# Turning four row sums by transposing transfers instead of TensorE

## Chip, core and metric

The kernel runs on one core of a Trainium2 chip. The metric is the device time of one execution in microseconds; the number before is the median of three runs. Engines: PE (TensorE), DVE (VectorE), ACT (ScalarE), POOL (GpSimd) and SP (SyncE), which here only issues transfers. PEld is TensorE's weight load.

## What is computed

```python
x  = A_q                                   # 1 x 2048 x 1024, float32
xn = layernorm(x)                          # over the 1024 columns
conv = long causal convolution of (short causal convolution of k) * v, per channel, plus a skip term
ffn  = silu(xn @ w1) @ w2                  # w1 1024 x 3584, w2 3584 x 1024
out  = x + xn * conv + ffn
```

The feed-forward part is nearly all of TensorE's work. The convolution is done by Fourier transforms (small matmuls on TensorE, butterflies on DVE).

## The kernel before, in words

Float32 products are made of three float16 products: each operand is split into a high half (ACT writes it) and a low rest (DVE writes it); this pair of instructions is the helper `split`. Lines L359 (ACT) and L351 (DVE) are helper lines through which all of these run.

The first matmul takes x in two row halves of 1024 rows. For most columns of w1 it uses a recursive scheme with seven products instead of eight (`PRODUCTS`). Its left operands are quarters of the normalised x, turned so that columns lie on partitions (`A11`, `A12`, `A21`, `A22`), and four sums of them, `S1` to `S4`. Each lies in one place `x0` to `x7` in SBUF as four row parts of 128 x 512: `S3` in x7, `S2` in x6, `S1` in x0, `S4` in x1, `A11` in x2, `A12` in x3, `A21` in x4, `A22` in x5.

For the first row half, `x_rows` adds the sums in place on DVE: row tiles xt4 to xt7 become `S3` and `S1`, then xt0 to xt3 become `S2` and `S4`. `transposes` turns each 128 x 512 part by four TensorE transposes into a PSUM tile `ft` (three of them in a ring), from which `split` writes high and low halves into the place. For the second half, `more_sums` splits the rows as they lie into a buffer `s`, `spill` stores them in DRAM (`xsp...`), and `load_x` reads them back much later by a transposing transfer (`X`, L341).

The order of all instructions is made when the program is built, by a list scheduler (`Order`). Generators yield operations with an estimated length; at each step the one with the earliest start minus its stream's bias is emitted. Each engine, and SP's queue, then runs its own list in order. `feed_forward` is one generator, so TensorE's matmuls of that part have a fixed sequence: two "plain" column blocks on the first half (48 matmuls of 256 columns with four row parts each, then 48 of 512), the same two blocks on the lower quarters (96 matmuls of 512 columns), then units of seven products of 12 matmuls. The products of the first unit go in the order P1 (`A11`), P7 (`S3`), P6 (`S2`), P2 (`A12`), P5 (`S1`), P1 of the next unit, P3 (`S4`), P4 (`A22`).

```python
PRODUCTS = {"P1": ("A11", "B11"), "P7": ("S3", "T3"), "P6": ("S2", "T2"), "P2": ("A12", "B21"),
            "P5": ("S1", "T1"), "P3": ("S4", "B22"), "P4": ("A22", "T4")}
XPLACE = dict(A11=2, A12=3, A22=5, S1=0, S2=6, S3=7, S4=1)
```

The right operands come from w1: `raw` tiles are loaded, their squares summed on ACT, factors formed on DVE and split into the ring `wo`.

Of the kernel before, what the change touches and what calls it, by code (L numbers as in the profile page):

```python
# [13 lines left out]
F16 = mybir.dt.float16  # L14
# [6 lines left out]
P = 128  # L21
# [6 lines left out]
KH = KD // 2  # L28
# [7 lines left out]
XS = 512.0  # L36
# [21 lines left out]
NC = len(PLAIN) // 4  # L58
W2PLACE = [(2, 6, 4, 0, 3), (1, 5, 7, 2, 6)]
FPLACE = (4, 0, 3, 1, 5, 7, 2, 6)  # L60

FACTORS = (("B11",), ("T2", "T3"), ("B21", "B22"), ("T4", "T1"))

# [53 lines left out]
class Order:  # L117
# [27 lines left out]
    def add(self, gen, bias, floor=0.0):  # L145
        s = Stream(gen, bias, floor)
        self.streams.append(s)
        self.advance(s)
# [151 lines left out]
def h3_ffn_kernel(ctx, tc, x, kp, vs, fs, shift, dskip, w1, w2, cfwd, cinv, out):  # L300
# [3 lines left out]
    add = order.add  # L304
    flag = defaultdict(Token)
# [12 lines left out]
    def size(a):  # L318
        n = 1
        for s in a.shape[1:]:  # L320
            n *= s
        return n
# [7 lines left out]
    def T(f, o, ins, us, m=0.1):  # L330
        return Op("PE", us, 0.3, f, ins, [o], m)
# [2 lines left out]
        n = size(o) * o.shape[0] * mybir.dt.size(o.dtype)  # L334
        return Op("SP", 0.4, 0.1, lambda: nc.sync.dma_start(o, i), [i], [o], m, n)

    def X(o, i, m=0.3):

        n = size(o) * o.shape[0] * mybir.dt.size(o.dtype)
        k = 1.2 if i.space == bass.MemoryType.DRAM else 3.0  # L340
        return Op("SP", 0.65 + n / 240e3, 0.1, lambda: nc.sync.dma_start(o, i, transpose=True), [i], [o], m, k * n)  # L341

    def G(o, i, m=0.3):
# [3 lines left out]
    def v_tt(o, a, b, op, **k):  # L347
        return V(lambda: nc.vector.tensor_tensor(o, a, b, op=op), o, [a, b], **k)  # L348

    def v_stt(o, a, s, b, op0, op1, **k):  # L350
        return V(lambda: nc.vector.scalar_tensor_tensor(o, a, s, b, op0=op0, op1=op1), o,  # L351
                 [a, b] + ([] if isinstance(s, float) else [s]), **k)

    def a_act(o, i, func, scale=1.0, bias=None, total=None):
        def f():
            kw = {} if bias is None else {"bias": bias}
            if total is not None:
                kw["accum_out"] = total
            nc.scalar.activation(o, i, func, scale=scale, **kw)  # L359
        ins = [i] + [s for s in (scale, bias) if s is not None and not isinstance(s, float)]  # L360
        p = A(f, o, ins)
        p.table = func if func in (AF.Silu, AF.Sqrt) else None
        p.busy += 0.07 * (len(ins) - 1) - 0.06 * (i.space == bass.MemoryType.PSUM)
        if total is not None:
            p.busy += 0.19
            p.writes.append(total)
        return p

    def split(hi, lo, src, scale, after=()):

        yield a_act(hi, src, AF.Copy, scale)
        yield v_stt(lo, src, scale, hi, MUL, SUB)
        for t in after:
            t.set()
# [56 lines left out]
    xst_r = Halves(order, lnp, "s", 6)  # L431
# [79 lines left out]
    xts, xns, xo = {}, {}, [{}, {}]  # L511
# [71 lines left out]
    def factor(name):  # L583

        if name == "A21":
            return second["A21"]
        return xo[0][name]

    def turned(src, tok, name, i, bias):

        yield ft.ready
        pt, ptok = ft.tile([P, KH, P])

        def mm():
            for c in range(KH):
                nc.tensor.transpose(pt[:, c, :], src[:, c * P:(c + 1) * P], ident)  # L596
        yield T(mm, pt, [src], 0.44, m=0.3)
        flag["turned", name, i].set()
        if tok is not None:
            tok.set()  # L600
        o = factor(name)[:, i]
        after = (ptok, flag["x", 0, name]) + ((flag["rows", i],) if name in ("A11", "A12") else ())
        add(split(o[:, :, 0], o[:, :, 1], pt, XS, after), bias)

    def transposes():
        for n, name in enumerate(("A11", "A12")):
            xo[0][name], xtok[0][name] = places[XPLACE[name]].tile([P, 4, KH, 2, P], F16)
        for i in range(4):
            yield flag["xn", i]
            x, _ = xns[i]  # L610
            yield from turned(x[:, 0:W], None, "A11", i, 0.2)
            yield from turned(x[:, W:], None, "A12", i, 0.2)
        second["A21"], second["tok"] = places[4].tile([P, 4, KH, 2, P], F16)
        for name in ("A22", "S2", "S3", "S1", "S4"):
            r = places[XPLACE[name]]
            yield r.ready
            xo[0][name], xtok[0][name] = r.tile([P, 4, KH, 2, P], F16)
        for i in range(4):
            yield flag["xn", 4 + i]
            z, _ = xns[4 + i]  # L620
            yield from turned(z[:, 0:W], None, "A21", i, 0.14)
            yield from turned(z[:, W:], None, "A22", i, 0.14)
        for name, low, q in (("S3", 4, 0), ("S2", 0, 0), ("S1", 4, 1), ("S4", 0, 1)):
            for i in range(4):
                yield flag["summed", name, i]
                x, tok = xns[low + i]
                yield from turned(x[:, q * W:(q + 1) * W], tok, name, i, 0.11)

    def x_rows():
        for i in range(4):  # L630
            for name in ("A21", "A22"):
                yield flag["turned", name, i]
            x, z = xns[i][0], xns[4 + i][0]
            yield v_tt(z[:, W:], z[:, 0:W], z[:, W:], ADD)
            flag["summed", "S1", i].set()
            yield v_tt(z[:, 0:W], x[:, 0:W], z[:, 0:W], SUB)
            flag["summed", "S3", i].set()
        for i in range(4):
            x, z = xns[i][0], xns[4 + i][0]
            yield v_tt(x[:, 0:W], z[:, W:], x[:, 0:W], SUB)  # L640
            flag["summed", "S2", i].set()
            yield v_tt(x[:, W:], x[:, W:], x[:, 0:W], SUB)
            flag["summed", "S4", i].set()
        yield 0.02
        for i in range(4):
            yield from more_sums(i)
        flag["x done"].set()
# [303 lines left out]
    def steps(o, w, xf, first, last, more=False):  # L951

        for k in range(KH):
            def mm(k=k):
                kw = dict(skip_group_check=more)
                nc.tensor.matmul(o, w[:, 0, k], xf[:, :, k, 0], start=first and k == 0, stop=False, **kw)  # L956
                nc.tensor.matmul(o, w[:, 0, k], xf[:, :, k, 1], start=False, stop=False, **kw)  # L957
                nc.tensor.matmul(o, w[:, 1, k], xf[:, :, k, 0], start=False, stop=last and k == KH - 1, **kw)  # L958
            yield T(mm, o, [w[:, :, k], xf[:, :, k]], 3 * (size(o) / 2400 + 0.003))
# [343 lines left out]
    def norms_w2():  # L1303
# [18 lines left out]
        for h in range(2):  # L1322
            for c in range(NC):
# [6 lines left out]
                for a in (0, 2):  # L1330
                    i = PLAIN[4 * c + a] // 2
                    raw, tok = yield from next_w2()
                    add(split(wc[:, a:a + 2, 0, :], wc[:, a:a + 2, 1, :], raw, tau[:, i:i + 1], (tok, flag["w2", h, c])), 0.05)
        yield places[FPLACE[0]].ready
        hold, ktok = places[FPLACE[0]].tile([P, NQ, W], F32)
        at = iter(FPLACE[1:])

# [602 lines left out]
```

## Time and profile before

| | |
|---|---|
| median of 3 runs | 1242.98 us (1242.75 to 1246.18) |
| profiled execution | 1248.08 us, span 1246.2 us |
| PE busy | 1233.9 us (99%) |
| DVE busy | 1108.8 us (89%) |
| ACT busy | 777.4 us (62%) |
| mean granted TensorE clock | 0.998 |
| moved by DMA | 275.62 MB, mean 221 GB/s |

The profile is of a single execution. Rows of a timeline give start, length, engine, line, operation and tiles; brackets hold the idle time just before an instruction and what ended it. Ends of matmuls are modelled: back to back, matmuls of 512 columns start every 0.216 us though each is listed with 0.38 us. Rows by stretch give, for each engine, busy time and the number of instructions, then the granted clock, the share of the DMA engines' time and GB/s.

### The profile page before, as it was taken

To read this page: it belongs to the slowest core of one execution; us is meant where nothing else is said; L and a number is where in the kernel's file an instruction comes from. 1 tells how busy PE (TensorE), PEld (TensorE's weight loads), DVE (VectorE), ACT (ScalarE), POOL (GpSimd) and SP (SyncE) were. 2 spreads that over 40 slices of the span, in tenths; PEclk is the share of its full clock that TensorE was granted. 3 is DMA by queue.
4 is the path that set the end of the run, shared out by engine and by line. 5 is a ranking of instruction groups with operands and counts; after the bars stand their busy time and mean duration, and the time that the engine had idled before them with its cause. 6 is when DMAs were issued, how large, how long until landed. Compare 5 with 4: busy or idle time off the path is not lost.

```text
span 1246.2 us, 16970 instructions
## 1 busy us (share of the span) xinstructions
PE 1233.9 (99%) x6092; PEld 602.5 (48%) x6092; DVE 1108.8 (89%) x1252; ACT 777.4 (62%) x1361; POOL 83.3 (7%) x93
## 2 busy tenths in 40 slices
PE   9999999999999999999999999999999999999998
PEld 8544444444444544445444544544454454445444
DVE  7999987997999769998899799889979979997992
ACT  7768987886687977559743732654273374545233
POOL 0000000000000000000000000000030130113114
PEclk9999999999999999999999999999999999999999
DMA  9368889789999888869986466389576766787777
GB/s 366 102 229 275 310 306 333 234 256 222 258 337 290 254 284 286 240 188 298 299 280 176 121 224 178 110 261 308 131 140 193 177 126 185 184 167 115 167 137 102
DMA packets 265028, 275.62 MB, mean 221 GB/s; under 512 B 72944, under 2 KB 191984, under 8 KB 263664
## 3 DMA queue, kind: packets, MB, share of 16 engines
q1 hardware_dynamic: 249216, 258.02, 67.2%
q0 software_dynamic: 15728, 16.52, 10.3%
q8 instruction: 47, 0.77, 0.3%
q14 instruction: 37, 0.30, 0.1%
HBM read 171.46 MB, written 88.34 MB: 208 GB/s over the span
## 4 chain that ended last, share of the span: by engine, by line
PE 87%; DVE 7%; DMA 3%; ACT 2%; issue 1%; SPq 0%; DVEq 0%; ACTq 0%
PE ff L956 13%; PE ff L957 13%; PE ff L958 13%; PE ff L1099 13%; PE ff L1101 13%; PE ff L1100 13%; DVE spec L348 2%; PE ps L1601 2%; DMA wraw<-in_w 2%; PE ps L1603 2%; PE ps L1602 2%; DVE tmp L348 1%; DVE x L351 1%; PE ft L596 1%; PE py L1790 1%
## 5 line engine op out<-in xcount | busy, mean ns | idle before, releaser
L1099 PE MATMUL ff<-x,wo 128*128 128x512 f16 x868 | 328.1, 378 | 1.5 <-ACT hf L359 0.7
L1101 PE MATMUL ff<-x,wo 128*128 128x512 f16 x868 | 328.1, 378 | 0.0
L1100 PE MATMUL ff<-x,wo 128*128 128x512 f16 x868 | 328.1, 378 | 0.0
L956 PE MATMUL ff<-x,wo 128*128 128x512 f16 (+1 forms) x808 | 303.3, 375 | 0.0
L957 PE MATMUL ff<-x,wo 128*128 128x512 f16 (+1 forms) x808 | 303.1, 375 | 0.0
L958 PE MATMUL ff<-x,wo 128*128 128x512 f16 (+1 forms) x808 | 303.1, 375 | 0.0
L348 DVE TENSOR_TENSOR spec<-spec 128x1024 f32<-128x1024 f32 (+2 forms) x232 | 259.4, 1145 | 2.1
L1101 PEld LDWEIGHTS <-wo 128*128 128x128 f16 x868 | 84.9, 98 | 101.6
L1099 PEld LDWEIGHTS <-wo 128*128 128x128 f16 x868 | 85.8, 99 | 99.2
L1100 PEld LDWEIGHTS <-wo 128*128 128x128 f16 x868 | 84.9, 98 | 101.1 <-issue 2.2
L958 PEld LDWEIGHTS <-wo 128*128 128x128 f16 x808 | 79.1, 98 | 92.4 <-issue 0.6
L956 PEld LDWEIGHTS <-wo 128*128 128x128 f16 x808 | 80.6, 100 | 88.2 <-issue 0.7
L957 PEld LDWEIGHTS <-wo 128*128 128x128 f16 x808 | 79.1, 98 | 88.3 <-issue 0.7
L348 DVE TENSOR_TENSOR tmp<-spec 128x2048 f32<-128x2048 f32 (+1 forms) x48 | 92.4, 1932 | 0.9
L359 ACT ACTIVATE spec<-spec 128x1024 bf16<-128x1024 f32 x32 | 33.7, 1054 | 68.5 <-DVE spec L348 68.5
L351 DVE SCALAR_TENSOR_TENSOR ht<-hf,wsc,ht 128x1024 f16<-128x1024 f32 (+1 forms) x56 | 67.4, 1203 | 10.0 <-ACT ht L359 9.7
L351 DVE SCALAR_TENSOR_TENSOR sig<-kin,taps,sig 128x1024 f32<-128x1024 f32 x48 | 61.4, 1280 | 12.0 <-ACT sig L359 12.0
L351 DVE SCALAR_TENSOR_TENSOR wo<-raw,wsc,wo 128x1024 f16<-128x1024 f32 (+1 forms) x56 | 64.0, 1146 | 8.7 <-ACT wo L359 8.6
L359 ACT ACTIVATE wo<-raw,wsc 128x1024 f16<-128x1024 f32 (+1 forms) x56 | 57.9, 1034 | 13.5 <-DVE raw L348 8.2
L345 POOL DMA_DIRECT2D out<-hf x44 | 39.5, 903 | 344.8 <-ACT hf L359 201.1
L359 ACT ACTIVATE ht<-hf,wsc 128x1024 f16<-128x1024 f32 (+1 forms) x56 | 60.8, 1086 | 2.0 <-DMA hsfA<-ht 0.3
L348 DVE TENSOR_TENSOR spec<-tmp 128x512 f32<-128x512 f32 (+1 forms) x80 | 60.7, 793 | 1.0
(187 smaller groups left out, 1707.3 us busy)
## 6 DMA issues: line engine op xcount, KB each, us to landing
wo<-hs SPq DMA_DIRECT2D x160, 256.0 KB, 3.5
hs<-ht SPq DMA_DIRECT2D x80, 256.0 KB, 4.5
raw<-in_w SPq DMA_DIRECT2D x28, 512.0 KB, 5.5
wraw<-in_w SPq DMA_DIRECT2D x24, 512.0 KB, 5.8
w2n<-in_w SPq DMA_DIRECT2D x24, 512.0 KB, 6.6
ws_T<-wo SPq DMA_DIRECT2D x22, 512.0 KB, 5.4
kin<-in_kp SPq DMA_DIRECT2D x16, 704.0 KB, 6.2
wo<-ws_T SPq DMA_DIRECT2D x22, 512.0 KB, 4.6
```

Source lines behind the costliest of these rows:

```text
L345: return Op("POOL", 1.1, 3.0, lambda: nc.gpsimd.dma_start(o, i, accum_op=ADD), [i], [o], m, 2.3 * n)
L348: return V(lambda: nc.vector.tensor_tensor(o, a, b, op=op), o, [a, b], **k)
L351: return V(lambda: nc.vector.scalar_tensor_tensor(o, a, s, b, op0=op0, op1=op1), o, [a, b] + ([] if isinstance(s, float) else [s]), **k)
L359: nc.scalar.activation(o, i, func, scale=scale, **kw)
L956: nc.tensor.matmul(o, w[:, 0, k], xf[:, :, k, 0], start=first and k == 0, stop=False, **kw)
L957: nc.tensor.matmul(o, w[:, 0, k], xf[:, :, k, 1], start=False, stop=False, **kw)
L958: nc.tensor.matmul(o, w[:, 1, k], xf[:, :, k, 0], start=False, stop=last and k == KH - 1, **kw)
L1099: nc.tensor.matmul(po, hx[:, n, 0, :], wc[:, n, 0, :], start=first and n == 0, stop=False, **kw)
L1100: nc.tensor.matmul(po, hx[:, n, 0, :], wc[:, n, 1, :], start=False, stop=False, **kw)
L1101: nc.tensor.matmul(po, hx[:, n, 1, :], wc[:, n, 0, :], start=False, stop=last and n == 3, **kw)
L1601: nc.tensor.matmul(o, cf[:, 0], h, start=i == 0, stop=False, **kw)
L1602: nc.tensor.matmul(o, cf[:, 0], l, start=False, stop=False, **kw)
```

## The change

`transposes` skips all four sums. `x_rows` instead adds a stream `shipped` for each row tile after its sums: it splits the whole row of two sums (128 x 1024) into a buffer `s` with rows on partitions, and `across` then turns each sum's part by one transposing transfer from SBUF to its place in SBUF. The streams have biases of 0.2 (`S3`), 0.15 (`S2`) and 0.1. The estimate of such a transfer's length can now be given by the caller.

```diff
+SHIPPED = ('S3', 'S1', 'S2', 'S4')
+URGENT = dict(S3=0.2, S2=0.15)
...
-    def X(o, i, m=0.3):
+    def X(o, i, m=0.3, k=None):
...
-        k = 1.2 if i.space == bass.MemoryType.DRAM else 3.0
+        k = k or (1.2 if i.space == bass.MemoryType.DRAM else 3.0)
...
         for name, low, q in (("S3", 4, 0), ("S2", 0, 0), ("S1", 4, 1), ("S4", 0, 1)):
+            if name in SHIPPED:
+                continue
             for i in range(4):
...
+    def shipped(names, i, src, toks):
+
+        def steps():
+            yield xst_r.ready if len(names) == 1 else xst_r.pairs
+            rows, rtok = (xst_r.tile if len(names) == 1 else xst_r.pair)([P, len(names) * KH, 2, P], F16, len(names))
+            yield from split(rows[:, :, 0], rows[:, :, 1], src.rearrange("p (k w) -> p k w", w=P), XS, toks)
+            for n, name in enumerate(names):
+                add(across(name, i, rows[:, n * KH:(n + 1) * KH], rtok), URGENT.get(name, 0.1))
+        add(steps(), URGENT.get(names[0], 0.1))
+
+    def across(name, i, rows, tok):
+
+        yield lambda: name in xo[0]
+        yield X(xo[0][name][:, i].rearrange("p k h w -> p (k h) w"), rows.rearrange("p k h w -> p (k h w)"), k=1.5)
+        tok.set()
+        flag["x", 0, name].set()
...
             flag["summed", "S3", i].set()
+            shipped(('S3', 'S1'), i, z, (xns[4 + i][1],) * 2)
...
             flag["summed", "S4", i].set()
+            shipped(('S2', 'S4'), i, x, (xns[i][1],) * 2)
```

Because the scheduler lays everything out anew, the order moves on every engine. Three places matter below.

TensorE, from the norm of a w1 tile (nm) to the first plain block on the lower quarters (ff1 from x4). Before:

```order
L489 MATMUL nm_656<-ss0_442,one_155 128x2
L596 MATMUL ft0_678<-ident_157,xt7_251 128x128 x4
L596 MATMUL ft1_686<-ident_157,xt7_251 128x128 x4
L596 MATMUL ft2_693<-ident_157,xt4_240 128x128 x4
L596 MATMUL ft0_705<-ident_157,xt5_244 128x128 x4
L956 LDWEIGHTS wo0_172
L956 MATMUL ff1_708<-x4_471,wo0_172 128x512
```

The same place now:

```order
L492 MATMUL nm_659<-ss0_442,one_155 128x2
L599 MATMUL ft0_684<-ident_157,xt7_251 128x128 x4
L599 MATMUL ft1_693<-ident_157,xt7_251 128x128 x4
L980 LDWEIGHTS wo0_172
L980 MATMUL ff1_707<-x4_471,wo0_172 128x512
```

Two transpose groups of `S3` (rows xt4 and xt5) stood ahead of the block; the other fourteen stood between its matmuls and those of the three blocks after it. All sixteen are gone.

DVE, at the same time: evacuations of `ft` to x4 and x5, the row additions, and now the split of a whole row into s1. Before:

```order
L348 TENSOR_TENSOR xt6_248<-xt2_225,xt6_248 128x512
L348 TENSOR_TENSOR xt7_251<-xt7_251 128x512
L351 SCALAR_TENSOR_TENSOR x4_471<-ft0_678,x4_471 128x4x128
L351 SCALAR_TENSOR_TENSOR x5_472<-ft1_686,x5_472 128x4x128
L348 TENSOR_TENSOR xt7_251<-xt3_228,xt7_251 128x512
L348 TENSOR_TENSOR xt0_201<-xt4_240,xt0_201 128x512
```

Now:

```order
L351 TENSOR_TENSOR xt6_248<-xt6_248 128x512
L354 SCALAR_TENSOR_TENSOR x4_471<-ft0_684,x4_471 128x4x128
L354 SCALAR_TENSOR_TENSOR x5_472<-ft1_693,x5_472 128x4x128
L354 SCALAR_TENSOR_TENSOR s1_193<-xt5_244,s1_193 128x8x128
L351 TENSOR_TENSOR xt6_248<-xt2_225,xt6_248 128x512
L351 TENSOR_TENSOR xt7_251<-xt7_251 128x512
```

The last evacuation to x4 comes after fewer additions, but the split into s0 (not in this piece) has moved ahead of the evacuations before it, and more splits stand between the additions.

SP's queue, between the first store of finished blocks (hs0) and the second pair of w1 loads (raw0). Before, with the stores of w1 factors (ws2) between:

```order
L335 DMA hs0_73<-ht1_182 128x4x256 x2
L335 DMA xt4_820<-in_x 128x1024
L335 DMA ws2_B11_77<-wo1_173 128x1024
L335 DMA xt5_852<-in_x 128x1024
L335 DMA xt6_861<-in_x 128x1024
L335 DMA xt7_869<-in_x 128x1024
L335 DMA ws2_T2_78<-wo4_176 128x2048
L335 DMA ws2_B21_79<-wo5_177 128x2048
L335 DMA hs1_74<-ht0_181 128x4x256 x2
L335 DMA raw0_942<-in_w1 128x4x256
```

Now (the last seven of the sixteen transposing transfers, and what is behind them):

```order
L344 DMA_TRANSPOSE x6_473<-s5_197 128x8x128
L344 DMA_TRANSPOSE x1_581<-s4_196 128x8x128
L344 DMA_TRANSPOSE x6_473<-s0_192 128x8x128
L344 DMA_TRANSPOSE x1_581<-s5_197 128x8x128
L344 DMA_TRANSPOSE x6_473<-s1_193 128x8x128
L344 DMA_TRANSPOSE x1_581<-s0_192 128x8x128
L344 DMA_TRANSPOSE x1_581<-s1_193 128x8x128
L338 DMA hs0_73<-ht1_182 128x4x256 x2
L338 DMA hs1_74<-ht0_181 128x4x256 x2
L338 DMA xt7_764<-in_x 128x1024
L338 DMA raw0_869<-in_w1 128x4x256
```

The transfer that completes `S2` (x6 from s1) is the fourteenth of the sixteen; two stores, a row load and the w1 loads stand behind the last.

## The prediction

> **What bounds the kernel now.** I read the page first, then the busy time by stretch.
>
> ```profile
> span 1246.2 us, 16970 instructions
> PE 1233.9 (99%) x6092; PEld 602.5 (48%) x6092; DVE 1108.8 (89%) x1252; ACT 777.4 (62%) x1361; POOL 83.3 (7%) x93
> ```
>
> ```profile
> core 0: us, PE busy (x) PEld busy (x) DVE busy (x) ACT busy (x) POOL busy (x), PEclk, DMA share, GB/s
> 20.00:40.00 20.00, 20.00 (x147) 14.70 (x145) 18.15 (x46) 19.81 (x33) 0.00 (x0) 1.00 0.86 311
> 40.00:60.00 20.00, 18.48 (x108) 11.04 (x106) 19.79 (x33) 13.79 (x27) 0.00 (x0) 1.00 0.16 36
> 60.00:80.00 20.00, 20.00 (x110) 10.96 (x108) 19.30 (x32) 15.11 (x27) 0.00 (x0) 1.00 0.90 293
> ...
> 400.00:500.00 100.00, 97.89 (x474) 46.55 (x472) 80.90 (x91) 80.79 (x147) 0.00 (x0) 0.98 0.85 276
> 1200.00:1246.00 46.00, 41.39 (x227) 21.97 (x225) 20.98 (x26) 17.64 (x34) 16.72 (x17) 0.98 0.71 107
> ```
>
> TensorE (PE) sets the time: it is idle for only 1246.2 - 1233.9 = 12.3 us, of which 4.6 lie at the very end. Work taken from it is time won, unless it waits instead. The work removed lies in 40 to 70 us, where DVE is nearly full too (19.8 and 19.3 of 20) and DMA almost empty at first (0.16). So whether DVE and the transfers deliver the sums in time decides.
>
> **The change, part by part.** The groups of instructions of the first 260 us, shapes apart, give the prices (xcount, busy us, mean ns, idle before):
>
> ```profile
> L351 DVE SCALAR_TENSOR_TENSOR x<-ft,x 128x512 f16<-128x512 f32 x32 | 20.3, 681 | 0.5 <-ACT x L359 0.5
> L359 ACT ACTIVATE x<-ft 128x512 f16<-128x512 f32 x32 | 17.4, 592 | 3.1 <-PE ft L596 2.8
> L351 DVE SCALAR_TENSOR_TENSOR s<-xt,s 128x1024 f16<-128x1024 f32 x12 | 14.4, 1217 | 0.0
> L359 ACT ACTIVATE s<-xt 128x1024 f16<-128x1024 f32 x12 | 12.4, 1045 | 0.6 <-DVE xt L348 0.6
> ```
>
> The timeline of PE:
>
> ```profile
> 38.64 1.47 PE L596 MATMUL ft<-ident,xt 128*128 128x128 f32 x12
> 42.52 1.82 PE L596 MATMUL ft<-ident,xt 128*128 128x128 f32 x12 [0.34 <-DVE x L351]
> 45.51 0.63 PE L596 MATMUL ft<-ident,xt 128*128 128x128 f32 x4 [1.18 <-DVE x L351]
> 45.98 0.38 PE L956 MATMUL ff<-x,wo 128*128 128x512 f16 x1
> 47.06 0.38 PE L956 MATMUL ff<-x,wo 128*128 128x512 f16 x1
> 52.67 0.38 PE L958 MATMUL ff<-x,wo 128*128 128x512 f16 x1
> ```
>
> *Removed from PE.* Between the rows at 47.06 and 52.67 stand 26 matmul starts: 0.216 us each, so a product of twelve takes 2.59 and a unit of seven 18.1. From the row at 45.51 to the matmul at 45.98 a transpose group of four takes about 0.44 (0.47 with the step). Sixteen go: 7.0 us. But the groups of xt4 and xt5 stand at 42.52 to 45.98, around two waits for DVE, ahead of the block that needs x4. They fill time in which PE waits. Fourteen stand between matmuls: 14 x 0.437 = 6.1 us on the path.
>
> *Does that block still start at 46?* It needs the last x4 evacuation from DVE. DVE before:
>
> ```profile
> 37.37 1.83 DVE L351 SCALAR_TENSOR_TENSOR x<-ft,x 128x512 f16<-128x512 f32 x3
> 41.69 1.88 DVE L351 SCALAR_TENSOR_TENSOR x<-ft,x 128x512 f16<-128x512 f32 x3
> 44.68 1.28 DVE L351 SCALAR_TENSOR_TENSOR x<-ft,x 128x512 f16<-128x512 f32 x2
> ```
>
> One operation of 512 columns takes 0.6 back to back, one of 1024 takes 1.2. Following the new DVE order from 37.4: half a statistics step 0.6 and the split of s0 1.2 come first, so the three evacuations end at 41.0, not 39.2. Another half 0.6, an addition 0.6, a small step 0.1 and three evacuations: 44.1. Two additions 1.3 and the x4 evacuation 0.6: 46.0. PE starts the block at about 46.05: as before, with two groups fewer done in its waits. PE now finishes a plain block first, turns three parts from 40.6 to 41.9, and needs evacuated `ft` tiles (42.9, 43.5) for the two groups of xt7: it stands still from 42.0 to 43.0 and from 44.0 to 46.05, with 0.9 us of transposes between. Then 96 matmuls (20.7) and a norm (0.14) lead to P1 of the first unit: 66.9 now; before, with fourteen groups more, 72.95. ACT's timeline confirms the latter, as it waits for the last plain block until 73.17, and shows that ACT has room for its share:
>
> ```profile
> 51.80 0.69 ACT L359 ACTIVATE hf<-ff,wsc 128x512 f32<-128x512 f32 x1 [3.94 <-PE ff L958]
> 73.17 0.69 ACT L359 ACTIVATE hf<-ff,wsc 128x512 f32<-128x512 f32 x1 [2.16 <-PE ff L958]
> ```
>
> *Splits.* Sixteen pairs of 592 and 681 ns become eight of 1045 and 1217: ACT saves 1.1 us, DVE 1.2 us. Neither is on PE's path after 46; I cost them at nothing, covered by the 20.7 us of matmuls.
>
> *Do the turned sums arrive?* DVE after 46.0 by the new order: x5 0.6, s1 1.2, four additions and small steps 2.8, s2 1.2, which ends at 51.85. To the last split (s1, second use) come one addition, s3, two additions, a factor split 0.7, s4, two additions, s5, four additions, two factor splits of 1.2, s0 and s1: 14.9 more, 66.8. The transfers cost SP's queue the following. Nearest are transposing transfers from SBUF of 128 KB (`sig`) and from DRAM of 1 MB (`x`), first by duration on SP (ns min/median/max), then by time to landing:
>
> ```profile
> L341 SPq DMA_TRANSPOSE sig<-cm x56: 1194/1247/2267, 373.2 to 1098.0; - x56
> L341 SPq DMA_TRANSPOSE x<-xspS x4: 4341/5908/8738, 272.1 to 306.5; - x4
> ...
> sig<-cm SPq DMA_TRANSPOSE x56, 3.3
> x<-xspS SPq DMA_TRANSPOSE x4, 8.3
> ```
>
> The new ones move 256 KB. On the line between the medians (1.25 at 128 KB, 5.91 at 1024) that is 1.9 us on SP and 4.0 to landing. Below: 1.25, if size doesn't matter. Above: 4.0, if SP holds each until it lands. I take 1.9, nearest to the 128 KB row, which also starts in SBUF. Per transfer I add 0.2 for an ordinary load standing between early ones: the fifth starts at 52.05, after s2; the fourteenth, which completes `S2`, at 52.05 + 9 x 1.9 = 69.15 and lands at 73.15. `S3`'s last, the sixth, lands by 58, far ahead of P7 at 69.5. P6 wants `S2` at 66.9 + 5.2 = 72.05. So this transfer is at the edge: up to 1.1 us of wait.
>
> The Trainium skill ("DMA: Bandwidth & Descriptors", "Latency and other measured facts") gives transposing transfers 261 GB/s with a non-contiguous middle dimension; by that, my estimate for 256 KB is 1.0 us, and the wait would be nil. The trace's 1247 ns for 128 KB on SP, about 105 GB/s, does not agree.
>
> *The clock.* A wait costs more than its length here. PE's timeline at the longest hole, and two stretches after it:
>
> ```profile
> 439.18 0.38 PE L958 MATMUL ff<-x,wo 128*128 128x512 f16 x1
> 441.68 0.38 PE L1601 MATMUL ps<-sig,cfw 128*128 128x512 f16 x1 [2.11 <-DVE spec L348]
> ...
> 445.73 0.38 PE L958 MATMUL ff<-x,wo 128*128 128x512 f16 x1
> ```
>
> ```profile
> 443.00:444.00 1.00, 1.00 (x4) 0.32 (x3) 0.47 (x1) 1.00 (x3) 0.00 (x0) 0.50 0.64 195
> 446.00:448.00 2.00, 2.00 (x11) 0.92 (x10) 0.00 (x0) 0.50 (x2) 0.00 (x0) 1.00 0.68 217
> ```
>
> After 2.1 us idle the granted clock fell to 0.50: ten starts took 4.05 us for 2.16, so 1.9 lost beside the hole. In 40 to 60 the waits before (0.34 and 1.18) left the clock at 1.00. The new ones are 1.0 and 2.05 with 0.9 us of work between, and the longer alone is about as long as the hole at 440. I count 1.9 us for it. Then P6 is wanted at 73.95 and `S2` is there.
>
> *Behind the transfers on SP.* Two stores, a row load and the w1 loads for the third unit wait for the last three transfers:
>
> ```profile
> 69.62 3.42 SPq L335 DMA_DIRECT2D raw<-in_w  x2
> 89.46 0.71 ACT L359 ACTIVATE wo<-raw,wsc 128x512 f16<-128x512 f32 x1
> ```
>
> They move from 69.6 to 69.15 + 3 x 1.9 + 2.4 = 77.3, 7.7 later. Their first factor was split at 89.5 and is wanted by P1 of the third unit, two units after 72.95: 109. Now 97 against 103: covered by 6 us, and no cost. If the transfers took 4.0 each, this cover would be gone as well.
>
> **Sum.** -6.1 (fourteen groups) + 1.9 (half clock) + 0 (`S2`) = -4.2 us. Profiled, 1248.08 - 4.2 = 1243.9; the median lies 5.1 below the profiled time, so 1242.98 - 4.2 = **1238.8 us**. A measurement of this kernel can tell some 0.3% (3.7 us) from no change; faster, same and slower below mean that.
>
> **Rivals.**
> - *The clock stays up* (18%). The Trainium skill ("TensorE: Matmul & The Clock Gate", "Why this matters for your kernels") warns only of gaps over some 3 us; by that, no gap here halves the clock. The trace's 2.1 us hole did. But the new waits are split by work, and the pair before passed. Then 1.9 is not paid, P6 waits 1.1: -5.0, 1238.0.
> - *A later hole closes* (8%). Everything behind is reordered, and the one at 440 costs 2.1 + 1.9 = 4.0. Gone, it gives 1234.8.
> - *New holes later* (27%). The same reordering can open one. PE reaches the convolution 4 us sooner while DVE, over 80% full there, has only 1.2 us less to do. For it: the hole at 440 is itself a wait for DVE. Against it: in 12.3 us of idle time there is no second one like it, and the same scheduler laid out both orders. One such hole: 1242.8; two: 1246.8.
> - *Transfers too slow: slower than before* (19%). If SP holds each until it lands (4.0), the fourteenth starts at 52.05 + 36 = 88.05 and lands at 92.05. P6 then waits 20 us: +13.9, with the half clock 1.9 +15.8, so 1258.8. It turns on the time per transfer d: the wait is 10d - 17.95; with the clock's 1.9 the gain is gone at d = 2.2, and slower by 3.7 needs 2.6. Twice the 128 KB row is 2.5; the row's own maximum is 2.27. Against it: the 128 KB row holds SP for 1.25 at the median while landing takes 3.3, so SP doesn't wait for landing there.
>
> **How the numbers follow.** The forecast has 28%. Faster: 24 of these 28, 16 of the 18, all 8 and 5 of the 27: 53%. Slower: 6 of the 27 (two holes) and 16 of the 19: 22%. Same: the rest, 25%. The range starts at 1233.0 (the hole at 440 gone and no half clock) and reaches 1248.0 (two new holes and a short wait at P6); outside stay most of the slow transfers.
>
> **What would show it.** Right: 64 transposes of L596 fewer; P1 of the first unit about 67 to 69, ACT's wait for the plain blocks ending there; a granted clock of 0.5 somewhere in 46 to 50; PE idle of 3 in 42 to 46; transposing transfers of 1.6 to 2.2 us on SP; no PE wait over 1 us for a transfer to x6. Wrong: a wait of PE on x6 or on wo between 70 and 110, transfers over 2.4 us, or PE idle in total above 17 us.

## The result: 1250.1 us, slower by 0.47%

| | before | after |
|---|---|---|
| median | 1243.55 us (6 runs, 1242.75 to 1246.18) | 1250.1 us (6 runs, 1248.66 to 1250.81) |
| profiled execution | 1248.08 us, span 1246.2 us | 1249.66 us, span 1247.7 us |
| ratio | | 1.0047, 95% interval 1.0036 to 1.0057 |

The forecast was 1238.8 us (1233.0 to 1248.0), faster. It was wrong in sign, and the result lies outside the range. The hole of 4.0 us at 440 us in the profile of before was particular to that execution: a fresh run of before (1243.21 us, span 1241.3) hasn't got it. Below, "before" in comparisons of traces is that fresh run (b0). In all timelines below, rows in between that no reading needs are left out.

The page of the changed kernel, and its stretches:

```profile
span 1247.7 us, 16839 instructions
PE 1229.1 (99%) x6028; PEld 595.2 (48%) x6028; DVE 1108.0 (89%) x1244; ACT 772.8 (62%) x1353; POOL 83.4 (7%) x93
```

```profile
40.00:60.00 20.00, 17.87 (x87) 9.09 (x86) 19.75 (x31) 16.86 (x28) 0.00 (x0) 0.91 0.49 85
60.00:80.00 20.00, 15.74 (x68) 6.75 (x67) 18.39 (x26) 8.99 (x14) 0.00 (x0) 0.90 0.96 208
```

The 64 transposes are gone and PE is busy 4.8 us less, but where 60 to 80 us was full (20.00) PE now stands for 4.3 us. The longest of PE's waits names the cause (in total, times, longest), and its timeline the places:

```profile
PE ff L980 <- DMA x<-s: 4.3, 1, 4.3
```

```profile
43.01 1.16 PE L599 MATMUL ft<-ident,xt 128*128 128x128 f32 x8 [0.77 <-DVE x L354]
44.55 0.38 PE L980 MATMUL ff<-x,wo 128*128 128x512 f16 x1 [0.38 <-ACT x L362]
45.91 0.59 PE L981 MATMUL ff<-x,wo 128*128 128x512 f16 x1 [0.98 <-DVE x L354]
67.99 0.38 PE L980 MATMUL ff<-x,wo 128*128 128x512 f16 x1
77.59 0.59 PE L980 MATMUL ff<-x,wo 128*128 128x512 f16 x1 [4.26 <-DMA x<-s]
```

P1 of the first unit starts at 67.99 (before: 73.0), P7 passes, and P6 waits 4.26 us for `S2` in x6. The granted clock fell twice, behind the small waits at 43 to 46 and behind this long one (in these rows by stretch the clock is the third number from the right):

```profile
46.00:47.00 1.00, 1.00 (x3) 0.32 (x3) 1.00 (x2) 1.00 (x3) 0.00 (x0) 0.50 0.00 0
80.00:82.00 2.00, 2.00 (x6) 0.76 (x5) 0.00 (x0) 0.00 (x0) 0.00 (x0) 0.50 1.14 342
```

Why `S2` is late stands in the timeline of SP's queue, next to that of DVE:

```profile
50.39 0.35 SPq L338 DMA_DIRECT2D xt<-in_x  x1
50.78 4.71 SPq L344 DMA_TRANSPOSE x<-s  x2
55.66 0.46 SPq L338 DMA_DIRECT2D xt<-in_x  x1
56.16 4.23 SPq L344 DMA_TRANSPOSE x<-s  x2
60.55 0.46 SPq L338 DMA_DIRECT2D xt<-in_x  x1
61.06 17.48 SPq L344 DMA_TRANSPOSE x<-s  x12
81.63 1.15 SPq L338 DMA_DIRECT2D raw<-in_w  x2
```

```profile
37.99 1.21 DVE L354 SCALAR_TENSOR_TENSOR s<-xt,s 128x1024 f16<-128x1024 f32 x1
48.97 1.27 DVE L351 TENSOR_TENSOR xt<-xt,xt 128x512 f32<-128x512 f32 x2
53.03 0.69 DVE L351 TENSOR_TENSOR xt<-xt,xt 128x512 f32<-128x512 f32 x1
58.82 0.69 DVE L351 TENSOR_TENSOR xt<-xt,xt 128x512 f32<-128x512 f32 x1
```

The first row of sums is split by 39.2, yet its transfers start at 50.78. Ahead of all sixteen on SP stands a reload (`xt4_637<-in_x`): it overwrites xt4, which the `S2` addition of row 0 still reads, and that ends on DVE at 50.2. This is SP's one long wait for such an addition, 15.1 us. The split gives the tile free for the scheduler; nothing counted the later reader. Two more reloads stand between the transfers and overwrite xt5 and xt6, read at 53.0 and 58.8; here those reads are over when SP gets to them, but the second transfer of each pair is long, 3.32 and 2.94 us where 1.3 is usual. The Trainium skill ("DMA: Bandwidth & Descriptors", "Anatomy of one DMA — SWDGE (gpsimd) path") says, in a section on transfers from GpSimd, that a wait for a semaphore happens on the issuing sequencer before dispatch; this trace agrees for SP: the reload starts 0.15 us behind the addition, and all that is queued behind it is held too.

### The profile page after: what moved, and what is told of

Same layout as the page of the kernel before. It is cut to its first block, busy times and chain, and to the rows that moved or that the text cites. A ratio compares the mean times of both kernels' runs of the same rounds, so it can differ in the third digit from the quotient of the medians.

```text
span 1247.7 us, 16839 instructions
## 1 busy us (share of the span) xinstructions
PE 1229.1 (99%) x6028; PEld 595.2 (48%) x6028; DVE 1108.0 (89%) x1244; ACT 772.8 (62%) x1353; POOL 83.4 (7%) x93
## 4 chain that ended last, share of the span: by engine, by line
PE 59%; DVE 8%; issue 4%; POOL 1%; DMA 1%; ACT 0%; SPq 0%; POOLq 0%; ACTq 0%; DVEq 0%
PE ff L1123 11%; PE ff L1125 11%; PE ff L1124 11%; PE ff L980 6%; PE ff L981 6%; PE ff L982 6%; DVE spec L351 3%; PE ps L1625 2%; PE ps L1627 2%; PE ps L1626 2%; POOL out L348 1%; DVE tmp L351 1%; PE py L1814 1%; PE py L1815 1%; PE py L1813 1%
```

## The experiments

One measure serves for all. The feed-forward matmuls come in the same sequence in every kernel, so each can be paired with its counterpart in before. The table gives start minus start in before, in us, for matmuls that start there at the times in the head (73.0 is P1 of the first unit; negative is earlier). These offsets are of the one profiled execution, the medians of all, and the two can differ: by 1.9 us in e1, 3.6 in e12. The labels are explained one by one below.

| kernel | 73.0 | 80.8 | 99.0 | 203.5 | 345.8 | 1236.9 (last) | median us | ratio, 95% interval |
|---|---|---|---|---|---|---|---|---|
| after | -5.01 | 1.90 | 2.06 | 2.06 | 3.61 | 5.17 | 1250.1 | 1.0047, 1.0036 to 1.0057 |
| a0 | -6.72 | 0.38 | 0.38 | 0.38 | 1.49 | 2.48 | 1246.05 (1 run) | |
| e1 | -6.66 | -6.66 | -6.67 | -4.16 | -1.31 | 0.71 | 1245.76 | 1.0011, 0.9997 to 1.0024 |
| e2 | -3.14 | -1.85 | -0.52 | -0.66 | -0.66 | 1.19 | 1245.09 | 1.0013, 1.0003 to 1.0022 |
| e4 | -6.43 | -4.40 | -3.76 | -2.86 | -1.69 | 3.56 | 1245.09 | 1.0010, 1.0000 to 1.0019 |
| e3 | -7.13 | -5.10 | -4.46 | -3.60 | -3.64 | 2.79 | 1245.28 | 1.0014, 1.0005 to 1.0022 |
| e11 | -5.02 | -5.02 | -3.28 | -2.51 | -0.71 | 0.86 | 1245.12 | 1.0012, 1.0004 to 1.0021 |
| e12 | -6.17 | 0.96 | 0.96 | 2.76 | 4.20 | 6.94 | 1247.52 | 1.0031, 1.0019 to 1.0043 |
| e13 | -6.22 | -6.22 | -6.23 | -6.37 | -2.25 | -0.77 | 1243.43 | 0.9999, 0.9990 to 1.0008 |
| e14 | -6.66 | -6.66 | -2.23 | -1.59 | 0.80 | 3.11 | 1246.29 | 1.0017, 1.0008 to 1.0026 |
| e5 | -2.22 | -2.21 | -2.22 | -0.41 | 4.72 | 7.45 | 1248.91 | 1.0042, 1.0028 to 1.0055 |
| e6 | -6.42 | -6.42 | -6.42 | -5.39 | 1.31 | 7.21 | 1250.15 | 1.0052, 1.0039 to 1.0064 |
| e7 | -6.86 | 27.51 | 27.51 | 30.11 | 43.22 | 58.94 | 1302.64 | 1.0472, 1.0458 to 1.0487 |
| e8 | 7.32 | 18.96 | 19.21 | 19.21 | 19.87 | 20.42 | 1263.7 | 1.0163, 1.0149 to 1.0177 |
| e9 | -1.15 | 17.66 | 17.65 | 17.66 | 18.44 | 19.19 | 1263.13 | 1.0158, 1.0144 to 1.0172 |
| e10 | -0.60 | 4.59 | 13.17 | 13.17 | 13.17 | 14.99 | 1257.71 | 1.0111, 1.0098 to 1.0125 |
| r1 | 1.36 | 1.37 | 1.50 | 1.36 | 11.21 | 18.52 | 1262.48 | 1.0154, 1.0140 to 1.0167 |
| r2 | 0.22 | 0.22 | 0.22 | 0.22 | 0.22 | 0.46 | 1243.8 | 1.0003, 0.9994 to 1.0012 |

**Before again (b0).**

> The kernel before, unchanged, for a second profile. The first profiled execution took 1248.1 where other executions took 1243 to 1244. If its 2.1 us wait at 440 us and the half clock behind it (4.0 together) were particular to that execution, this one has no such hole and a span near 1241; if they belong to the kernel, the hole stands at the same place.

It had no hole at 440 us and no wait of PE over 1.2 us.

### Is it the reload on SP?

**Free the row tile later (e1).** The token is set once by the split and once behind the `S2` addition:

```diff
-            shipped(('S3', 'S1'), i, z, (xns[4 + i][1],) * 2)
+            shipped(('S3', 'S1'), i, z, (xns[4 + i][1],))
...
             flag["summed", "S2", i].set()
+            xns[4 + i][1].set()
```

> The changed kernel, but the row tiles xt4 to xt7 count as free only after the second use (the S2 addition reads them), so that their reloads no longer stand ahead of transposing transfers that are ready. Theory (the reloads hold up SP's queue until 50.4, 55.7 and 60.6 us, so that S2 lands after 77 us): the twelfth or fourteenth transfer lands before P6 wants it near 71 to 73, PE's 4.3 us wait on x6 and the half clock behind it (2.1) go, P1 of the first unit stays at 68, and the kernel takes 1250.1 - 6.5 = 1243.6, or some 1.5 less if nothing is lost later. Rival (the transfers themselves are slow or disturb the loads): SP still issues them until 75 us or later, the wait on x6 stays above 3 us, 1248 to 1251.

SP's timeline of e1:

```profile
39.02 10.97 SPq L344 DMA_TRANSPOSE x<-s  x4
50.10 0.52 SPq L338 DMA_DIRECT2D xt<-in_x  x1
51.20 18.65 SPq L344 DMA_TRANSPOSE x<-s  x12
```

The transfers start at 39, one reload is left between them, the wait on x6 is gone, and PE is 6.66 us ahead at P1. The median, 1245.76, is still 2 us above the theory: the lead was lost further on, mostly in waits of 2.48 us at 199, 1.66 at 342 and 2.01 at 897 us; below.

**Half of the sums (e2), and the split begun later (e4).**

```diff
-SHIPPED = ('S3', 'S1', 'S2', 'S4')
+SHIPPED = ('S3', 'S1')
...
-            shipped(('S2', 'S4'), i, x, (xns[i][1],) * 2)
```

> The changed kernel with only S3 and S1 turned by transfers; S2 and S4 go by TensorE as before. The reloads still stand ahead in SP's queue and the split of s0 still stands ahead of the evacuations. Theory: eight transpose groups (3.5 us) come back on PE, P1 of the first unit at 71.5, S3 and S1 arrive in time (last transfer landed by 70, P7 wants it at 74), no wait on x6, half clock at 46 stays: 1250.1 + 3.5 - 6.5 = 1247 or a little less. Rival (any eight or more transposing transfers cost the gain by themselves, through DVE or the DMA engines): no faster than 1250.

```diff
         def steps():
+            yield flag["x", 0, "A22"]
             yield xst_r.ready if len(names) == 1 else xst_r.pairs
```

> The changed kernel, but no row is split for transfer until the parts of A22 are split, so that the split of s0 no longer stands ahead of the evacuations to x4 and x5. Theory (that split made PE wait at 42 to 46 and halved its clock): PE waits there as before (1.5 us in total), the clock stays at 1.00 in 44 to 50, the first plain block on the lower quarters has its matmuls at full speed and P1 of the first unit comes 1.5 to 2 us earlier, at 66.3. The splits of the second use of s0 and s1 come later on DVE (about 69 and 71), so S2 lands near 74 and PE waits 2 to 3 us for it, with a half clock: 1246 to 1250 in all. Rival (the half clock has another cause than that wait): clock 0.5 at 46 to 49 again.

e2 keeps the reloads ahead of its eight transfers and yet PE waits for none, since `S2` goes by PE; eight groups give 3.14 at P1 (8 x 0.437 = 3.5). The half clock at 46, which the theory kept, did not come in this execution. In e4 PE waits 1.87 us on x6 and no longer, and the clock stays at 1.00 behind it. Both medians are 1245.09.

**Both edits of e1 and e4 (e3).**

> The changed kernel with both edits that took the wait away: row tiles freed at the second addition, splits begun after A22 is turned. Theory: no wait on x6, P1 of the first unit 6.4 to 6.7 us ahead; the end anywhere from 1238 to 1248, since it is one more order with holes of its own. Rival (the lead lasts where SP and DVE are both free): still over 5 us ahead at 350 us, 1237 to 1240.

7.13 us ahead, 1.87 lost on x6 as in e4 though none was expected, and 3.64 still there at 346; at the end it is 2.79 behind.

**The same order, reloads moved on SP alone (e11, e12).** e1 laid out everything anew. In e11 every engine keeps the changed kernel's order; only three reloads are issued behind the sixteenth transfer. In e12 only the first is.

```diff
-        yield L(xts[t][0], xr[t // T2, t % T2])
+        op = L(xts[t][0], xr[t // T2, t % T2])
+        if t in (10, 11, 14, 15) and len(sent) < 16:      # e12: if t == 10 and ...
+            held, op.emit = op.emit, lambda: held() if len(sent) > 15 else sent_then.append(held)
+        yield op
...
+        sent.append(name)                                 # in across, behind each transfer
+        if len(sent) == 16:
+            for f in sent_then:
+                f()
```

> The changed kernel with every instruction in its place, except that the three reloads of row tiles on SP's queue ahead of and between the sixteen transfers stand behind the last of them. Theory (these reloads alone hold the transfers): the first transfer starts at about 39 us, the wait on x6 at 73 is gone, P1 of the first unit stays 6.7 us ahead of the kernel before through the first unit, and the time falls by about 7 us against the changed kernel, to 1242 to 1244. Rival (TensorE's lead is lost again to waits for ACT, DVE and loads further on, since everything behind the sums is laid out for a later TensorE): the lead of 6.7 us at 100 us is under 3 us by 350 us, and the time is 1244 to 1248.

> As the run with three reloads behind the transfers, but only the first of them is moved; the other two still stand behind the second and the fourth transfer. Theory A (the first alone is the cause, an ordinary load between costs 0.2 us as predicted): no wait on x6, the time as with all three moved. Theory B (each reload waits for its DVE addition at 51 to 53 us, and the second transfer behind a load takes 2.7 to 3.3 us on SP for 1.3): the third transfer starts at about 52, the fifth at about 57 instead of 61.1, S2 lands at about 73, and TensorE waits 0.5 to 2 us on x6; the time is 1 to 3 us above that with all three moved.

SP's and ACT's timelines of e11, then SP's timeline and waits and PE's timeline of e12:

```profile
39.16 31.39 SPq L344 DMA_TRANSPOSE x<-s  x16
70.65 1.48 SPq L338 DMA_DIRECT2D xt<-in_x  x3
...
85.43 1.06 ACT L362 ACTIVATE junk<-raw 128x1024 bf16<-128x1024 f32 x1 [2.91 <-DMA raw<-in_w]
```

```profile
39.51 2.68 SPq L344 DMA_TRANSPOSE x<-s  x2
54.15 0.35 SPq L338 DMA_DIRECT2D xt<-in_x  x1
54.55 4.25 SPq L344 DMA_TRANSPOSE x<-s  x2
59.73 0.35 SPq L338 DMA_DIRECT2D xt<-in_x  x1
60.13 17.70 SPq L344 DMA_TRANSPOSE x<-s  x12
...
SPq L338 <- DVE xt L351: 12.6, 2, 11.8
...
76.86 0.59 PE L989 MATMUL ff<-x,wo 128*128 128x512 f16 x1 [4.69 <-DMA x<-s]
```

e11 settles where the wait comes from: three loads in other places on one queue, and it is gone (the transfer that completes `S2` lands at 69.36); the median is 5.0 us under the changed kernel's 1250.1 (before stood at 1243.5 both times). The forecast of 1242 to 1244 was missed all the same, and its rival was right on the end: the lead of 5.0 goes in pieces. 1.9 us of it go at 88 to 91, where ACT waits 2.91 us for a raw load that SP issued at 78.59 and only then does an evacuation that PE needs; 0.8 more go by 203.5, 1.8 by 346 and 1.6 behind. That the first reload alone did it is refuted by e12: it starts at 39.51 and waits as long, 4.69. SP then stands 11.8 us for the second addition, and the third reload starts at 59.73, ahead of the last twelve transfers. Theory B was right on the cause, but its fifth transfer at 57 was too early (60.13) and its wait of 0.5 to 2 us too short. (The profiled execution of e12, 1251.13 us, is the slowest of its six; the table's row is from it.)

**The changed kernel again (a0).**

> The changed kernel once more, unedited. Theory (the reload of xt4 on SP's queue holds the sixteen transposing transfers until the DVE addition that reads xt4): TensorE's wait on x6 comes again at 73 to 78 us, 3.5 to 4.5 us long, since it follows from the order; span 1246 to 1248. Rival (the wait is particular to one execution, as the 4.0 us hole at 440 us in the first profile of the kernel before was): no wait over 1 us on x6, span about 1243. The half clock at 46 to 49 us may or may not come: where the wait on x4 stays in two pieces of about 0.4 and 1.0 us it has come once and stayed out twice.

The wait came at the same place, 5.04 us (3.5 to 4.5 expected). The clock stayed at 1.00 from 46 to 49 this time, though the small waits were the same (0.76, 0.39, 0.98), and it is 1.7 us further ahead at P1. So the half clock cost some 1.45 us where it came (the other 0.26 lie ahead of it).

### Why is the lead of 6.7 us lost?

**Other orders (e5, e6, e7).** Each is e1 with one or two numbers changed, so that the same instructions stand in another order:

```diff
-        add(more_pairs(), 0.05)                                    # e5
+        add(more_pairs(), 0.3)
-        for gen, bias in ((loads(), 0.05), (load_v(), 0.04), ...   # e6
+        for gen, bias in ((loads(), 0.0), (load_v(), 0.0), ...
-URGENT = dict(S3=0.2, S2=0.15)                                     # e7
+URGENT = dict(S3=0.0, S2=0.1)
```

> The later free of the row tile as before, and the w1 tiles get a larger bias (0.3 for 0.05), so that their raw loads stand earlier on SP's queue at the start. Theory (the 6.7 us won by 67 us are given back to single later waits, in which ACT stands in order in front of a raw load that is late, ahead of a PSUM evacuation that TensorE needs): the loads from 70 to 250 us land earlier, TensorE does not stop by 2.5 us at 199 us, and the time is 1239 to 1243. Rival (TensorE ahead of the rest is stopped by the supply itself, whatever the order): the 6.7 us are lost by 350 us again in other waits, and the time is 1244 to 1247.

> The later free of the row tile as before, and the loads of the convolution (kf, v) lose their bias (0.05 and 0.04 become 0), so that they stand behind w1's loads where they compete. Theory (late raw loads behind the 1 MB of kf on SP's queue stop ACT at 192 to 198 us, and TensorE through it): the wait of ACT for raw at 197 us is under 3 us, TensorE's hole there under 1 us, the time 1239 to 1243.5. Rival (supply, or any other order has holes of its own): another hole of 1 to 3 us takes its place before 350 us, 1244 to 1247.

> The later free of the row tile as before, with URGENT 0 for S3 and 0.1 for S2 in place of 0.2 and 0.15: the same instructions, only another order from 45 us on. Both theories have P1 of the first unit 4 to 7 us earlier than in the kernel before, if S2 is still in time. If what is given back later is the chance of one order, the place of the holes after 170 us differs from that of the run with 0.2 and 0.15, and the time lies anywhere from 1238 to 1248. If it is the supply, the offset against the kernel before is back at 0 to +2 at the end, as there, and the time is 1244 to 1247.

PE's timeline of e6, then of e7:

```profile
263.65 0.39 PE L983 MATMUL ff<-x,wo 128*128 128x512 f16 x1 [1.92 <-DVE wo L354]
309.78 0.46 PE L1626 MATMUL ps<-sig,cfw 128*128 128x512 f16 x1 [2.08 <-ACT spec L362]
521.24 0.38 PE L981 MATMUL ff<-x,wo 128*128 128x512 f16 x1 [2.43 <-ACT hf L362]
```

```profile
86.43 0.59 PE L492 MATMUL nm<-ss,one 128*128 128x2 f32 x2 [17.54 <-ACT junk L362]
100.98 0.59 PE L981 MATMUL ff<-x,wo 128*128 128x512 f16 x1 [13.96 <-DMA x<-s]
```

My theory missed all three times. In e6 the hole at 199 did go, and 6.4 us of lead lasted to 180 us, 5.4 to 203; then other holes took it, as the rival said. e5 has the half clock at 47 and is no better behind it. e7 shows what the biases are for: transfers behind loads, and PE stands 31.5 us.

**The order of before, with the change in it (e8, e9, e10).** The transposes stay in the scheduler's plan, and are not issued; each split, at its old place, reads the row tile, and its transfer stands on SP behind it.

```diff
-        yield T(mm, pt, [src], 0.44, m=0.3)
+        ship = name in SHIPPED
+        yield T((lambda: None) if ship else mm, pt, [src], 0.44, m=0.3)
...
+        def low():
+            nc.vector.scalar_tensor_tensor(rows[:, :, 1], w, XS, rows[:, :, 0], op0=MUL, op1=SUB)
+            nc.sync.dma_start(o.rearrange("p k h w -> p (k h) w"), rows.rearrange("p k h w -> p (k h w)"), transpose=True)
```

> The kernel before with its order of instructions kept on every engine: the sixteen transpose groups of the sums stay in the scheduler's plan but are not emitted on TensorE; each of the sums' sixteen splits, at its old place, reads the row tile and writes rows, and its transposing transfer stands on SP behind it. Only the free of the row tiles, and so four reloads on SP, move by some places. Theory (the change itself is worth about 6 us, the first order had SP blocked, and the rest is lost to new holes that each new order brings): TensorE reaches P1 of the first unit 5 to 7 us earlier, no wait on x6, hardly a hole over 1 us after that, the time 1236.5 to 1239.5, ratio 0.995 to 0.997. Rival (TensorE runs into the supply of DVE, ACT and the transfers, whatever the order): the gain is lost in waits after 100 us and the time is 1242 to 1246.

e8 took its buffers from the ring; e9 takes twelve halves in turn:

```diff
-            got.extend(xst_r.tile([P, KH, 2, P], F16))
+            got.append(shaped(xst_r.whole[n % 6][:, n // 6 % 2 * W:][:, 0:W], [P, KH, 2, P], F16))
```

> As the run that keeps the order of before, but the sixteen splits go to twelve separate half buffers in turn (each used again only four transfers before the end), where that run reused a buffer whose transfer had just been issued: there ACT stood 7.78 us at 57.7 for a transfer, and DVE, SP, the raw loads and TensorE behind it. Theory (the change itself is worth 5 to 7 us once no engine waits for a buffer): ACT's wait is gone, P1 of the first unit comes 4 to 6.5 us earlier; behind it ACT's order has the squares of raw (issued at 69.7 before, about 73 now, behind the sixteen transfers) ahead of the evacuations, so TensorE may lose 2 to 6 us of its lead at 74 to 84 us; then no new hole over 1 us, since the order is the old one. Time 1237 to 1243. Rival (the sixteen transfers between the stores and loads hold SP's queue so long, whatever the buffers, that the raw loads come 10 us later): the wait for raw stays over 5 us, the time is above 1248.

e10 issues the four transfers of `S4`, and then the four reloads, behind the next two raw loads:

```diff
+            if (n, a) == (4, 1):
+                for f in waiting[0] + waiting[1]:
+                    f()
```

> As the run that keeps the order of before with twelve buffers, but on SP the four transfers of S4 and the four reloads stand behind the next raw loads, so that hardly a load stands between transfers. Theory (transfers of 1.3 us each leave the raw loads where they were, about 70 us): ACT's wait of 17.97 us for raw at 74 is gone, the time falls by 18 to 22 us to 1241 to 1245; P1 of the first unit is 4 to 7 us ahead, and TensorE loses most of that before 85 us, because ACT squares raw at 75 to 79 us in its order ahead of evacuations, and raw lands no sooner than before. Rival (the lead survives): P1 of the second unit 4 to 7 us ahead, 1237 to 1239.5.

SP's and ACT's timelines of e9, then SP's of e10:

```profile
67.07 1.24 SPq L628 DMA_TRANSPOSE x<-s  x1
68.98 0.49 SPq L337 DMA_DIRECT2D ws_T<-wo  x1
69.56 3.06 SPq L628 DMA_TRANSPOSE x<-s  x1
87.56 1.12 SPq L337 DMA_DIRECT2D raw<-in_w  x2
...
92.26 1.06 ACT L361 ACTIVATE junk<-raw 128x1024 bf16<-128x1024 f32 x1 [17.97 <-DMA raw<-in_w]
```

```profile
62.94 5.36 SPq L343 DMA_TRANSPOSE x<-s  x4
74.12 1.26 SPq L337 DMA_DIRECT2D raw<-in_w  x2
75.43 7.91 SPq L343 DMA_TRANSPOSE x<-s  x4
```

All three refute my hope that the old order would keep the gain. In it, sixteen transfers are spread among loads and stores, and SP is busy from 52 to 88 us; the raw loads go at 87.56 instead of 69.65, ACT waits 17.97 us for them with evacuations behind, and PE stands 16.8 us. With `S4` and the reloads out of the way the raw loads go at 74.12, but PE still waits three times (4.1, 3.4, 7.0 us), and e10 is 14.2 us slower than before. Behind 100 us, though, the three lose only 1.2 to 1.8 us more: in its own order the rest has hardly a hole, for a PE that comes late.

**New orders without the change (r1, r2).** The numbers of e5 and e6 put into before:

> The kernel before, without the change, with the larger bias (0.3 for 0.05) of the w1 tiles: the order alone is laid out anew. Theory (any new order has holes that the old one had not): 1244 to 1251, with new waits of TensorE over 1 us in the trace. Rival (new orders are as good as the old one where TensorE has the transposes to do): 1242 to 1244.5, no new wait over 1 us.

> The kernel before, without the change, with the loads of the convolution (kf, v) at no bias: a second new order. Theory as for the w1 bias: 1244 to 1251 with new holes after 170 us, none before. Rival: 1242 to 1244.5.

```profile
331.50 0.58 PE L956 MATMUL ff<-x,wo 128*128 128x512 f16 x1 [7.48 <-DVE hf L348]
606.20 0.58 PE L956 MATMUL ff<-x,wo 128*128 128x512 f16 x1 [4.94 <-DVE hf L348]
```

These are PE's two longest new holes in r1: an order alone cost 18.9 us. r2 fell to the rival: a new order need not cost anything (1.0003).

**Take single holes away on SP (e13, e14).** In e1, ACT waits 5.20 us at 192 for a raw load issued behind 1.7 MB (kin, kf), with an evacuation behind it; PE stands 2.48. Timelines of e1 for SP, ACT and PE:

```profile
182.87 0.43 SPq L338 DMA_DIRECT2D kf<-in_fs  x1
186.72 0.56 SPq L338 DMA_DIRECT2D raw<-in_w  x1
...
197.52 1.06 ACT L362 ACTIVATE junk<-raw 128x1024 bf16<-128x1024 f32 x1 [5.20 <-DMA raw<-in_w]
...
199.30 0.38 PE L981 MATMUL ff<-x,wo 128*128 128x512 f16 x1 [2.48 <-ACT x L362]
```

e13 issues kin and kf (and POOL's load of 0.5 KB into kf) behind that raw load; e14 is e11 with the reloads also behind the next two raw loads. Every other instruction keeps its place on its engine. An operation that is put off goes into `waiting`.

```diff
             yield L(raws[n][2][a], w1r[:, ks, cols])
+            while waiting:             # e13; e14: if (n, a) == (4, 1)
+                waiting.pop(0)()
```

> The run with the later free of the row tile, with two loads of the convolution (kin, kf; 1.7 MB) moved on SP from ahead of one raw load at 182 to 187 us to behind it; the rest of the order is unchanged. Theory (that load late behind them makes ACT wait 5.20 us at 192, and TensorE 2.48 us at 199): ACT's wait falls under 1.5 us, TensorE's hole at 199 goes, the lead is still 6 us at 300 us; of it some goes in the holes behind, which TensorE reaches 2.5 us sooner; time 1.0 to 2.5 us less than that run's 1245.8, so 1243 to 1245. Rival (supply): another wait of 1.5 to 2.5 us comes before 300 us, the time is unchanged.

> The changed kernel's order with the four reloads of row tiles behind the transfers and behind the next pair of raw loads too, instead of ahead of that pair. Theory (the raw loads, issued at 78.6 behind reloads and stores, made ACT and with it TensorE late at 88 to 91 by 1.9 us): the raw loads go at 72 to 76, no wait over 0.5 us at 85 to 95, the lead of 5 to 6.7 us lasts to 190 us; time 1 to 2 us under the 1245.1 of that run: 1243 to 1244.2. Rival: the lead is back at 3.3 by 190 us through another wait, 1245.

ACT and PE in e13:

```profile
192.67 1.05 ACT L362 ACTIVATE junk<-raw 128x1024 bf16<-128x1024 f32 x1
...
206.59 0.38 PE L991 MATMUL ff<-x,wo 128*128 128x512 f16 x1 [1.42 <-ACT hf L362]
```

The wait and the hole at 199 are gone, and the lead at 203.5 is 6.37 instead of 4.16. Part of it goes 3 us later (1.42), more at 341 (1.71) and 355 (0.65). The ratio goes from 1.0011 to 0.9999, level with before; the intervals of the two overlap, so the firm part is the hole in the trace. In e14 the raw loads do go at 72.6, but PE then waits 2.60 us at 87 for DVE: the rival was right there.

## Why the prediction was wrong, by its steps

- **Removed from PE: right.** -6.1 was predicted at P1 (14 groups x 0.437); -6.72 and -6.66 were measured where the clock stayed up. In a0 the offset grows by 6.14 from the second matmul of the block to P1, which is the fourteen groups; the other 0.58 is that this matmul starts at 45.64 instead of 46.22.
- **Half clock at 46: near in size, partly by luck, and not in every execution.** The reason given was one wait of 2.05 us; the longest wait there was 0.98. 1.9 predicted; 1.45 in the profiled one (from the matmul at 46.0 to the one at 51.6 it falls back 2.14 us, a0 with the same waits 0.69), and nothing in a0 and e1. The Trainium skill ("TensorE: Matmul & The Clock Gate", "Why this matters for your kernels") warns of gaps over some 3 us: here waits of 0.77, 0.38 and 0.98 us within 3.7 us did it here and in e11, and not in seven other profiled executions that have them.
- **Do the turned sums arrive: this step failed.** "Per transfer I add 0.2 for an ordinary load standing between early ones: the fifth starts at 52.05" took a reload for an instruction that only takes its place. It waits on SP for the last reader of the tile that it overwrites and holds the queue (the first to 50.39), and the second transfer behind it takes up to 3.32 us instead of 1.3: the fifth transfer started at 61.06, 9.0 us later than predicted, and the fourteenth, which completes `S2`, landed at 77.35, not at 73.15. The price of a transfer, on which I spent the working, was too high and gave some of it back, 1.31 us on SP (predicted 1.9) and 2.8 to landing (4.0). From the fifth to the fourteenth that is 13.5 us instead of 17.1, and 1.2 less to landing:

```profile
L344 SPq DMA_TRANSPOSE x<-s x16: 1237/1307/3317, 50.8 to 77.2; - x16
x<-s SPq DMA_TRANSPOSE x16, 2.8
```

  The step cost 4.26 of wait and about 2.6 of half clock behind it: from -5.01 to 1.90.
- **Behind the transfers on SP: not borne out where it counted.** The raw loads moved to 81.6 (77.3 predicted), and the offset stayed at 2.06 through 203 us. But there PE was 6 us later than predicted. In e11, where it kept its lead and the raw loads went at 78.6, they cost 1.9 us at 88 to 91. The prediction asked when the first factor is wanted; ACT's squares of raw, which stand in its order ahead of an evacuation for PE, need the loads sooner. In e1, with the loads at 74.0, nothing was lost by 99 us.
- **The rivals.** "Transfers too slow" named the place (P6 on x6), the sign and the clock's share, but not the mechanism: d was 1.31, far under the 2.2 from which it would decide. "A later hole closes" had nothing to close, as the hole at 440 us is not in b0. "New holes later" came too, in pieces: 1.55 at 255 to 347 us, a net 1.56 from there to the last matmul, and 1.2 behind it.
- **The sum** of the trace: -5.01 + 6.91 + 0.16 + 1.55 + 1.56 + 1.2 = 6.4, the difference of the spans (1247.7 - 1241.3).

Shown by one move on one queue (e11) is that the reloads cost about 5 of the 6.6 us. Shown for one hole, the one of e1 at 199 us, which went in e13 and in e6, is that a late load on SP, through ACT's order, takes part of the lead. That PE's lead must be lost in any order is not shown: none of the orders that ran kept it, and e13 came level. What an order would need to keep all 6.7 us stays open, as do the reason why the same waits halve the clock only sometimes, and why a transfer behind loads is longer (the last section has a pattern, not a cause).

## What to carry to other kernels

Work taken off the full engine is won only as far as the queue that takes it over is free: read that queue's order row by row, and ask of each load in it what it overwrites and who reads that last. A scheduler's "free" ahead of the last reader put one load in front of sixteen transfers and two between them. When nearly every instruction of the full engine is covered by an order that fits, an edit that lays the order out anew can cost more than the edit is worth; compare it with moves on one queue that leave the rest in place, before judging the idea itself.

## What the hardware showed that was not expected

- A transposing transfer of 256 KB from SBUF to SBUF holds SP for 1.24 to 1.31 us and lands in 2.8 us; at 128 KB it was 1.25, so size hardly counts between these two. The Trainium skill ("DMA: Bandwidth & Descriptors", "Issuing engines are not separate DMA queues") calls the time to initiate usually small beside the transfer; here it is nearly half of it, and for a plain 512 KB load as short as 0.35 us.
- Behind loads of 512 KB it is longer: up to 3.32 us for the second behind a 512 KB reload (4.71 for the pair, 4.25 in e12), 3.06 behind a load and a store in e9, 1.98 each for four behind two raw loads in e10, against 1.34 each for four in a row (5.36). Behind 256 KB stores it stayed at 1.29 to 1.31 (at 58.33 and 60.35 in e9). The landings show a pattern: in the changed kernel the second transfer behind each reload was done on SP at 55.49, 60.39 and 65.02, and these reloads landed at 56.02, 60.50 and 65.16. It was so in ten such pairs of a0, e2, e3, e4 and e12 too (2.2 to 3.2 us for the second transfer, done 0.1 to 0.5 us ahead of the landing), and not in the one of e5.
- The half clock came with each wait of 4.3 to 5.0 us on x6 (after, a0, e12) and lasted to between 80 and 83 us; behind the waits of 1.87 us on x6 (e3, e4) the clock stayed at 1.00. The small waits at 43 to 46 us (0.8, 0.4 and 1.0) stand in nine of the profiled executions and brought it in two of them, after and e11.
